# First softmax batch from scores with tokens as rows, and a new order for the first half

## The chip, the cores and the metric

One core of one Trainium2 chip. The metric is the device time of one execution in microseconds (us), lower is better. Three runs of the kernel before gave 615.01, 616.36 and 616.61 us, median 616.36. The core has TensorE (PE in the profile, with PEld for its weight loads), VectorE (DVE), ScalarE (ACT), GpSimd (POOL) and SyncE (SP, which here only issues transfers).

## The reference

Attention between 512 tokens and 32 states in both directions, for 8 batches of 8 heads, then a two-layer network with softplus on all 4608 rows:

```python
scores = scale * np.matmul(x, state.transpose(0, 1, 3, 2))
scores = scores - scores.max(-1, keepdims=True)
a = np.exp(scores)
a /= a.sum(-1, keepdims=True) + 1e-09
xread = np.matmul(a, state)
scores2 = scale * np.matmul(state, x.transpose(0, 1, 3, 2))
scores2 = scores2 - scores2.max(-1, keepdims=True)
a2 = np.exp(scores2)
a2 /= a2.sum(-1, keepdims=True) + 1e-09
sread = np.matmul(a2, x)
...
h = x @ w_in
g = np.maximum(h, 0.0) + np.log1p(np.exp(-np.abs(h)))
return (g @ w_out).astype(np.float32)
```

In the last three lines `x` is `xread` and `sread` with heads side by side: rows of 512, `w_in` 512 x 2048, `w_out` 2048 x 512. Batch 0 is `b == 0` below.

## The kernel before, in words

The first layer is folded into the attention: instead of `xread @ w_in` the kernel makes V = state x w_in once per batch (step v, `v_product`, L370) and multiplies it with the softmax weights `a` (step g, `gemm1`, L635). To do so it needs `a` with the pair (head, state) on the partitions and the tokens along the free axis. The scores (step Q, `scores`, L431) come out of TensorE in that form too: 32 states of 4 heads on 128 partitions, one bank of PSUM for even heads (e = 0), one for odd heads, 512 tokens along. The softmax of the tokens against the states, though, wants its maximum and sum over the 32 states of a head, so the steps of the first softmax go there and back:

- step 1, `a_turn` (L450): VectorE transposes blocks of 32 x 32 from PSUM into SBUF, so that the states lie along the free axis;
- steps 2 to 6: maximum (`a_max`, VectorE), subtraction (`a_sub`), exponential (`a_exp`, ScalarE), sum, epsilon and reciprocal (`a_sum`, VectorE), multiplication (`a_mul`); subtraction and multiplication are given to VectorE or GpSimd by a table;
- step 7, `a_back` (L497): VectorE transposes the blocks back.

Batch 0 goes in two halves of 256 tokens, because its tokens are loaded in two halves. The second softmax (over tokens, steps e, f, i, t, u) reads the same score banks: maximum on VectorE, exponential on ScalarE (step f), transposes by TensorE against an identity matrix (step t, `b<-ident,s` in rows), copies (u).

Batch 0 takes its first four tiles of 128 columns of the hidden layer (F1) in full float32 (`b<-s,s` in rows; TensorE does such a product in two passes, which the trace records as two matmuls), and its first two tiles of the second layer as well (`b<-d,s` of 128x512). All others are split into a high and a low part (steps h/l for V, 8/9 for `a`, m/n for the softplus, D/E for `w_out`) and take three passes in float32r. Weights come as 8-byte words: `a`, `b`, `c` (ScalarE, ScalarE or VectorE, VectorE) make float32 of the ten pieces of `w_in` and put it into the tile `W`; A, B, C do the same for `w_out`. From batch 1 on the second layer takes seven products of half-size slabs instead of eight (steps U, W, Y, F, H, L, M, k, q; M is the product on TensorE), whose weights are written to DRAM (j, K) and read back (J).

The order of everything is a string, PLAN (L43), of 1758 steps: a loop at L999 takes its letters one after the other and runs the next turn of that step, and the order in which instructions are issued is kept on every engine. The table ENG (L67) says for each turn of the steps that may run on more than one engine which one takes it. No engine overtakes within its own queue: an instruction that waits holds back all behind it. SyncE issues all loads and stores in one queue. Buffers are rooms of fixed sizes (`Rooms`), free again after a set number of uses: the r2 rooms are `s`, r4 `d`, r8 `g`, r1 `v`, the eight PSUM banks `b`.

Of the kernel before, what the change touches and what calls it, by code (L numbers as in the profile page):

```python
# [20 lines left out]
P = 128  # L21
# [23 lines left out]
    "1GB93elalGm9gCEgjnADanbEcGfgCGDsimbGIsGsEB4GcvAhjRUmWnS2CjhAlgnOGDlYGaKKgrg3EmsgmjTbBacBnnGCGGAsgjGjbC5Ocssjsv"
    "hjvmTUDGmEGlhlh4WhDdnlnAgYE5GUlBGjgKsOmnG6K7GmG6snQvWCYhDGAjleGjjj7hjlGmKEmj8Kg8SBgs991fnmGGgTCjDUntjnTJsjijWs"
    "tmgeGsUjYEGg1usj2fnGGuGKWoUoj2XtvjKvKpUWuhlQGoY1gshYJgseKogsghW2lsgYHKljsggghlsgsggUsKKfWLgsgsMsFXes3KiJ3FKYHs"
    "R4XFpyzHHLFKFrFMLHZLLHkpMJ5kJMHkJq4JLk5MMLJMkHLH6XJkH7PMR6vvFL7kHJrL8T98hMF9lJhMlhk1g2kgslkHghfsvlvLH3qysgL3h4"
    "lzhsPhLklgXMsghJsgglgH5ssLXJ4gsklqZggJHsMLsJqkgF5ggJssgMss6HkqMFsFkLtuHJFM6LHML7JMTFqH7tF8MkLPJMHkuLHJJM9dJRHP"
    "kvikLkvphFhLkyrkMqzPHXq8HJll9MhlJLLHgJLMZFkHMPhqLkslgkkJkkMHMvskhvQylPhJlggPsq1g2efgzPqskggesJLsqsgh1Hg3sZglhL"  # L50
    "M2ssXfJM3ltHkPkgF4gs5sgggssLsiJJFHs4HLFJ5MMLH6LuMFJJFHMFL6tvkFukHhLlvRP7HHPLhJrkqq8HkLlq7hhMJL9qJJMTH8kMJllMTJ"
    "XPLFqHLqkk9HLMMgggMMsHsskkqkkkLkJPPJJPTJJXPvQv1khhql2qlee13ggggssshsHfhf42llLgggMgggsHFqL35sss4ssgggMsssH56F6k"
    "LFHkLFH7MMttyF8HqFLu7L9kuzHkLFMJPJPJJMMMJJPPJPPRvHZkkHFqLiLkHh8vMMkLlrHhHhHqLlLlkkH9LLqMJXPTJPPJJJJMgMggMssshk"
    "kHkklkkvvQge1hfsgggshsshH2Lll3h1l2leLFgggg4sssfsggggssssgMMM3FHFqsH4F5FqqLH5Lqk6LTPPJJJPMtytMMJJXJHFFHkLiuk7kH"
    "HHHzL6HLqLZkukLMMkFMvvRJJPh8hH7kLqlq9LrqLh8MMMJTJPXJJJPPXJPl9kHkhkkklgMMskklkvQvgghqHl1ehe2sfhfLlh13lqgggssss4"
    "Lq253qgggwiMyPssgHs45MgJzlsgFPLstkuJgkxsgssgtgsMH6sqL7H86PuMFZRLvvkrFJkhlvhlPvhhFFJHFLhlh97MHLlHHMHLMwFkMkHJJ8"
    "hLJJJlPq9MHgLkxsgkgMFsslPwgHgLJqPkLghkMqMgxkHsskgPkskgLJgJgsllqsPLMHLHyzMqZsPwssMkgggqLggskg&P&wsxsxMgkqwkx%%s"
    "wgswx&xqP&%s%s&g%w&wP%wJsxxgwJxxw&x%&%sF&gFw&wx%&%qxg%wHx&s&Lg%H%&sL%&&%s%sHLHLMFHMHFPFJFHHkJFLFLFLLFJkHMLMFJk"
# [4 lines left out]
    '3': "PPPPDPPPDDDPDDDP",  # L63
    '6': "PPPDPPPDDPDDDPPP",
    '8': "DAPPADAAPAAAAADPDD",
    '9': "PPDPDDPDDPDDDPDDPP",
    'B': "DDAADAAA",  # L67
# [1 line left out]
    'E': "DDDDDDPD",
    'F': "DDPDDDDPDDPPDDPDPDPDPPDPDDPDPPDPPDPDPDDDPDPPDPPDDPDDDDPDDDDDDPDD",  # L70
    'H': "AAADAPPAPAPPADDAPAADADAAAAAAAAADPAAAADPAADDAPDAADADDPAADAAAPAPAPAAPADAAAPAPAAAAPADADAADAAAAAAAAPAAAAPAAADAAAAPAA",
    'L': "PDDDDDPDPDDPDDDDDDDDDPPDDDDPDDDDPPPPDPPPPPDDPDDDPDDPDPDDDPDDDPDDDPDDDDPDPDPDDPPDPPPPPPDDDDDDDDDDPDPDPDDDPDDDDPDD",
    'U': "DDPDPDDP",
# [1 line left out]
    'Y': "DDDDPDPD",
    'b': "AAAADDAAAA",
    'h': "AADDDDDAADAAADDDDAADDDDADDADAADDDADDADAADAAAADAAAAADADADADADDAAAAAAA",
    'k': "DADDDDDDDDDDDDDDAADDDDDDDDDDDDDDDADDDDDDDDDDDDDDAADDDDDDDDDDDDDDDDDDDDDDDDDDDDDDAADDDDDDDDDDDDDDAADDDDDDDDDDDDDDDDDDDDDD",
    'm': "PPDADDDAPAAPAA",
    'n': "DDDPDDDDPDPDPP",  # L80
    'o': "AADD",
    'q': "PDDPPDDDPDPDDPPDPPDDDDPPPPPPPDDPDDPPDDDPPPDDPDDDDPPPDPDPDDDD",
    'u': "DAADDAAAADDADDDD",
# [977 lines left out]
```

## Time and profile before

| what | value |
|---|---|
| median of three runs | 616.36 us |
| the profiled execution | 616.66 us |
| its span, first to last instruction | 614.7 us |
| PE busy | 598.5 us (97%) |
| DVE busy | 490.9 us (80%) |
| ACT busy | 267.8 us (44%) |
| POOL busy | 304.9 us (50%) |
| chain that ended last | 92% PE |
| DMA | 161.62 MB, mean 263 GB/s |

A page of the profile gives busy time of each engine, the span in 40 slices of 15.4 us, and the chain of work that ended last, followed back from the end. An engine with idle time costs nothing unless others wait for it; so the waits of the engine that is never idle are what to look for, and then the order of work that leads to each of them. Matmuls overlap, so that a row's time divided by its count is the pace, while the mean duration of one is longer.

### The profile page before, as it was taken

To read this page: it belongs to the slowest core of one execution; us is meant where nothing else is said; L and a number is where in the kernel's file an instruction comes from. 1 tells how busy PE (TensorE), PEld (TensorE's weight loads), DVE (VectorE), ACT (ScalarE), POOL (GpSimd) and SP (SyncE) were. 2 spreads that over 40 slices of the span, in tenths; PEclk is the share of its full clock that TensorE was granted. 3 is DMA by queue.
4 is the path that set the end of the run, shared out by engine and by line. 5 is a ranking of instruction groups with operands and counts; after the bars stand their busy time and mean duration, and the time that the engine had idled before them with its cause. 6 is when DMAs were issued, how large, how long until landed. Compare 5 with 4: busy or idle time off the path is not lost.

```text
span 614.7 us, 10410 instructions
## 1 busy us (share of the span) xinstructions
PE 598.5 (97%) x4048; PEld 485.1 (79%) x4048; DVE 490.9 (80%) x662; ACT 267.8 (44%) x416; POOL 304.9 (50%) x185
## 2 busy tenths in 40 slices
PE   2999999999999999999999999999999999999997
...
PEclk9999999999999999999999999999999999999999
...
GB/s 305 409 407 326 304 303 362 311 344 377 113 307 237 398 334 112 206 292 315 410 105 229 380 323 106 194 382 412 219 155 146 322 208 78 21 244 233 203 310 77
DMA packets 50415, 161.62 MB, mean 263 GB/s; under 512 B 4288, under 2 KB 29376, under 8 KB 37824
## 3 DMA queue, kind: packets, MB, share of 16 engines
...
## 4 chain that ended last, share of the span: by engine, by line
PE 92%; DVE 3%; DMA 3%; issue 1%; POOL 0%; SPq 0%; ACT 0%; POOLq 0%; DVEq 0%; ACTq 0%
PE b L103 92%; DMA slabs<-d 2%; DVE d L103 2%; DMA d<-in_xt_dram 1%; DVE s L103 1%; POOL s L103 0%; DVE v L103 0%; SPq L103 0%; ACT s L103 0%; DVE g L103 0%; DVE W L103 0%; POOLq L103 0%; DVEq L103 0%; ACTq L103 0%
## 5 line engine op out<-in xcount | busy, mean ns | idle before, releaser
L103 PE MATMUL b<-g,d 128*128 128x256 f32 (+1 forms) x1576 | 290.6, 337 | 0.1
L103 PEld LDWEIGHTS b<-g,d 128*128 128x128 f32 x1576 | 246.8, 190 | 36.2 <-POOL d L103 1.1
L103 PE MATMUL b<-d,d 128*128 128x512 f32 x744 | 177.3, 393 | 1.0 <-DVE d L103 1.0
L103 PEld LDWEIGHTS b<-d,d 128*128 128x128 f32 x744 | 137.9, 188 | 32.5 <-issue 2.4
L103 ACT ACTIVATE g<-b 128x512 f32<-128x512 f32 x112 | 66.2, 599 | 141.6 <-PE b L103 132.0
L103 DVE TENSOR_TENSOR s<-s,b 128x512 f32<-128x512 f32 (+1 forms) x105 | 68.7, 675 | 48.0 <-PE b L103 38.7
L103 POOL TENSOR_TENSOR d<-g,d 128x1024 fp32r<-128x1024 f32 x28 | 71.9, 2570 | 46.5 <-ACT d L103 19.6
L103 DVE TENSOR_TENSOR d<-g,d 128x1024 fp32r<-128x1024 f32 x56 | 88.2, 1580 | 3.0 <-ACT d L103 2.7
L103 PE MATMUL b<-g,s 128*128 128x512 f32 (+1 forms) x280 | 70.7, 370 | 0.0
L103 ACT CAST d<-g 128x1024 fp32r<-128x1024 f32 x53 | 55.4, 1052 | 33.5 <-POOL g L103 15.6
L103 PEld LDWEIGHTS b<-g,s 128*128 128x128 f32 x280 | 50.3, 188 | 11.6 <-issue 2.5
L103 POOL TENSOR_TENSOR s<-s 128x256 f32<-128x256 f32 x28 | 31.1, 1114 | 33.5 <-DVE s L103 28.1
L103 DVE TENSOR_TENSOR d<-b,d 128x512 fp32r<-128x512 f32 x62 | 41.6, 682 | 7.3 <-ACT d L103 6.9
L103 POOL TENSOR_TENSOR s<-s,v 128x512 f32<-128x512 f32 x19 | 22.8, 1201 | 44.9 <-DVE v L103 44.3
L103 ACT CAST d<-b 128x512 fp32r<-128x512 f32 x35 | 20.1, 590 | 49.5 <-PE b L103 49.3
L103 POOL TENSOR_SCALAR d<-g 128x1024 fp32r<-128x1024 f32 x17 | 26.6, 1569 | 29.9 <-DVE g L103 19.4
L103 POOL TENSOR_TENSOR g<-g,g 128x1024 f32<-128x1024 f32 x14 | 35.2, 2518 | 10.4 <-DVE d L103 7.7
L103 POOL TENSOR_TENSOR d<-d,d 128x1024 fp32r<-128x1024 f32 (+2 forms) x15 | 30.8, 2055 | 12.7 <-PE b L103 6.4
L103 PE MATMUL b<-W,ST 64*32 64x512 f32 (+2 forms) x544 | 32.7, 577 | 4.1 <-DVE W L103 4.1
L103 DVE TENSOR_TENSOR d<-d,d 128x1024 fp32r<-128x1024 f32 (+2 forms) x27 | 31.4, 1163 | 0.3
L103 DVE COPY s<-b 128x512 f32<-128x512 f32 (+2 forms) x30 | 16.2, 546 | 16.2 <-PE b L103 16.1
L103 ACT COPY s<-b 128x512 f32<-128x512 f32 (+2 forms) x27 | 13.7, 516 | 30.2 <-PE b L103 25.6
...
## 6 DMA issues: line engine op xcount, KB each, us to landing
g<-slabs SPq DMA_DIRECT2D x98, 1024.0 KB, 6.6
d<-in_xt_dram SPq DMA_DIRECT2D x16, 512.0 KB, 6.4
g<-in_w_out_dram SPq DMA_DIRECT2D x8, 1024.0 KB, 15.1
d<-in_xn_dram SPq DMA_DIRECT2D x16, 512.0 KB, 6.8
slabs<-d SPq DMA_DIRECT2D x16, 512.0 KB, 5.8
...
g<-in_w_in_dram SPq DMA_DIRECT2D x6, 1024.0 KB, 15.5
...
```

Of the source, the lines that this page charges most:

```text
L103: return lambda *a, **k: self.tc.keep_in_program_order(f(*a, **k))
```

## The change

For batch 0 the first softmax no longer takes its scores from step Q. Step 1 now makes them a second time on TensorE with the tokens as the stationary side: for each half 8 float32 matmuls, each with 128 tokens of one pair of heads as weights (128 x 128) and the pair's 64 columns of state as moving data. The states then lie along the free axis in a PSUM bank, and VectorE's maximum and subtraction read it there; the four block transposes go. Subtraction for batch 0 is VectorE's always. Back goes the half by four TensorE transposes into a PSUM bank (step 7), which a new step 0 (`a_copy`, on ScalarE by the table) copies to SBUF. The maximum and exponential of the second softmax still read step Q's banks, which therefore have two readers instead of four.

The first half of PLAN is another one (the last 881 letters are the same), and with it the table: counted up to the first M in either string, the steps that the table places stand 35 on POOL, 60 on DVE, 42 on ACT before, and 25 on POOL, 71 on DVE, 48 on ACT now. In the same stretch there are 424 letters before and 445 now. Order of the loads: the fourth `w_in` piece now comes ahead of the second half of batch 1's tokens, the first piece of `w_out` between two of `w_in`, and the first `xn` later.

```diff
 PLAN = (
-    "TSTSIITITIQI1IQ2O3e12e34dfbaafb4c565OOIIOc6vttQvahbuu7cabhXg8chve8Xh7hg9fbag1tahbgg8A8ccsB9sgCgvhguD2hsGsBOIAm"
...
+    "TSTSIITaII1T2Q3I4bQOae1fIebf2Oca3v5td46hc7ba0ihcu5vhQbOegt67Icv1Ohfg08eba9hAuIgahBSctgCbgcggUssgv8hushBm8lnG9s"
...
 ENG = {
...
-    'D': "PDDDPAAA",
...
-    'W': "PAAPPPPA",
...
+    'D': "APAAAADA",
...
+    'W': "AAAAADAD",
...
@@ -216,7 +217,7 @@
     def load_xT():
         for b, i in HALVES:
             if b == 0:
-                t = xT[b, i] = r4.take([P, 4, S // 2])
+                t = xT[b, i] = r4.take([P, 4, S // 2], uses=2)
                 nc.sync.dma_start(t.t, xt[b, :, :, S // 2 * i:S // 2 * i + S // 2])
             else:
                 t = xT[b, i] = r4.take()
@@ -433,8 +434,8 @@
             for u in range(2 if b == 0 else 1):
                 n = S // 2 if b == 0 else S
                 if u == 0:
-                    sc[b, 0], sc[b, 1] = [banks.take(uses=4 if b == 0 else 3) for _ in range(2)]
-                    few[b] = r1.take(uses=3)
+                    sc[b, 0], sc[b, 1] = [banks.take(uses=2 if b == 0 else 3) for _ in range(2)]
+                    few[b] = few.get(b) or r1.take(uses=3)
                 heads([sc[b, e][:, n * u:n * u + n] for e in range(2)], b, lambda q: xT[b, u][:, q] if b == 0 else xT[b, q // 2][:, q % 2])
                 xT[b, u].done()
                 if b:
@@ -447,26 +448,43 @@
     def flat(t):
         return t.rearrange("p a n -> p (a n)")
 
+    turned, back = {}, {}
+
     def a_turn():
         for b, i in KEYS:
-            t = T[b, i] = r2.take([P, 16, NS])
             if b == 0:
-                for e in range(2):
-                    nc.vector.transpose(flat(t[:, 8 * e:8 * e + 8]), sc[b, e][:, span(0, i)])
-                    sc[b, e].done()
+                few[b] = few.get(b) or r1.take(uses=3)
+                t = turned[i] = banks.take(uses=2)
+                for j in range(2):
+                    for q in range(4):
+                        nc.tensor.matmul(t[:, 256 * j:256 * j + 256].rearrange("p (e q n) -> p q e n", e=2, q=4)[:, q],
+                                         xT[b, i][:, q, P * j:P * j + P], ST0[:, 0, q].rearrange("p (e n) -> p e n", e=2),
+                                         start=True, stop=True)
+                xT[b, i].done()
             else:
+                t = T[b, i] = r2.take([P, 16, NS])
                 nc.vector.transpose(flat(t.t), sc[b, i].t)
                 sc[b, i].done()
             yield
 
+    def grouped(t):
+        return t.rearrange("p (a n) -> p a n", n=NS)
+
     def a_max():
         for k in KEYS:
-            nc.vector.tensor_reduce(mx(*k), T[k].t, AX.X, ALU.min if k[0] else ALU.max)
+            nc.vector.tensor_reduce(mx(*k), T[k].t if k[0] else grouped(turned[k[1]].t), AX.X, ALU.min if k[0] else ALU.max)
+            if k[0] == 0:
+                turned[k[1]].done()
             yield
 
     def a_sub():
         for k in KEYS:
-            elementwise(T[k].t, T[k].t, spread(mx(*k)), ALU.subtract, engine())
+            if k[0] == 0:
+                T[k] = r2.take([P, 16, NS])
+                nc.vector.tensor_tensor(T[k].t, grouped(turned[k[1]].t), spread(mx(*k)), ALU.subtract)
+                turned[k[1]].done()
+            else:
+                elementwise(T[k].t, T[k].t, spread(mx(*k)), ALU.subtract, engine())
             yield
 
     def a_exp():
@@ -496,9 +514,22 @@
 
     def a_back():
         for k in KEYS:
-            af[k] = r2.take(uses=4 + F1 if k[0] == 0 else 2)
-            nc.vector.transpose(af[k].t, flat(T[k].t))
+            if k[0] == 0:
+                t = back[k[1]] = banks.take()
+                for e in range(2):
+                    for j in range(2):
+                        nc.tensor.transpose(t[:, 256 * e + P * j:256 * e + P * j + P], flat(T[k].t)[:, 256 * j + P * e:256 * j + P * e + P], ident)
+            else:
+                af[k] = r2.take(uses=2)
+                nc.vector.transpose(af[k].t, flat(T[k].t))
             T[k].done()
+            yield
+
+    def a_copy():
+        for i in range(2):
+            af[0, i] = r2.take(uses=4 + F1)
+            cast(af[0, i].t, back[i].t, engine())
+            back[i].done()
             yield
 
     def part(b, i, e):
@@ -987,7 +1018,7 @@
         "a": win_upper, "b": win_lower, "c": win_join,
         "A": wout_upper, "B": wout_lower, "C": wout_join, "D": wout_hi, "E": wout_lo,
         "v": v_product, "h": v_hi, "l": v_lo,
-        "Q": scores, "1": a_turn, "2": a_max, "3": a_sub, "4": a_exp, "5": a_sum, "6": a_mul, "7": a_back,
+        "Q": scores, "1": a_turn, "2": a_max, "3": a_sub, "4": a_exp, "5": a_sum, "6": a_mul, "7": a_back, "0": a_copy,
         "8": a_hi, "9": a_lo, "e": s_max, "f": s_exp, "i": s_sum, "t": s_turn, "u": s_copy, "R": s_read,
         "r": s_scale, "y": s_back, "z": s_hi, "Z": s_lo,
         "w": w_hi, "x": w_lo, "g": gemm1, "&": h_copy, "%": h_add, "s": softplus, "m": g_hi, "n": g_lo, "G": gemm2,
```

On TensorE, from the program's start to the first product of the hidden layer, before (`b` are PSUM banks, `d0` and `d1` the two halves of batch 0's tokens, `ST0` its states, `ident` the identity; step Q, the products with `W` and batch 1's scores are among the rows left out):

```order
L103 MATMUL b0_1_97<-d0_1_78,ST0_72 32x256
...
L103 MATMUL b4_5_183<-ident_67,s2_3_140 128x128 x4
L103 MATMUL b5_6_188<-ident_67,s6_7_148 128x128 x4
...
L103 MATMUL b2_11_235<-s3_14_224,s9_10_216 128x256
L103 MATMUL b2_11_235<-s3_14_224,s2_17_231 128x256
```

The same stretch of TensorE's queue, from the program's start to the first product of the hidden layer and the transposes behind it, in the changed kernel:

```order
L104 MATMUL b0_1_99<-ST0_72,d0_1_78 128x2x32 x8
...
L104 MATMUL b3_4_142<-ST0_72,d1_2_81 128x2x32 x8
...
L104 MATMUL b6_7_182<-ident_67,s4_5_151 128x128 x4
L104 MATMUL b7_8_194<-ident_67,s1_2_121 128x128 x4
...
L104 MATMUL b4_13_244<-s0_13_203,s9_10_191 128x256
...
L104 MATMUL b7_14_247<-ident_67,s6_7_159 128x128 x4
L104 MATMUL b5_15_253<-ident_67,s8_9_167 128x128 x4
```

The products with the 64 columns of `ST0` (8 for each half) stand ahead of and behind the two halves of step Q, the transposes of batch 0's exponential (`ident` on `s4_5`) are followed by those of its softmax weights (`s1_2`), and of the second half both (`s6_7`, `s8_9`) stand behind the first product of the hidden layer.

On VectorE, from its first instruction on batch 0 on, before (`s0_1` and `s1_2` are the two halves of the first softmax, `v0_1` holds maxima and sums, `SCALAR_TENSOR_TENSOR` into `W` is the join of a weight piece):

```order
L103 STREAM_TRANSPOSE s0_1_110<-b0_1_97 128x256
L103 STREAM_TRANSPOSE s0_1_110<-b1_2_98 128x256
L103 TENSOR_REDUCE v0_1_99<-s0_1_110 128x16
L103 TENSOR_REDUCE v0_1_99<-b0_1_97 128x1
L103 TENSOR_SCALAR v0_1_99<-v0_1_99 128x1
L103 STREAM_TRANSPOSE s1_2_129<-b0_1_97 128x256
L103 STREAM_TRANSPOSE s1_2_129<-b1_2_98 128x256
L103 TENSOR_REDUCE v0_1_99<-s1_2_129 128x16
...
L103 SCALAR_TENSOR_TENSOR W_74<-s4_5_144,s3_4_142 128x4x128
L103 TENSOR_REDUCE v0_1_99<-s0_1_110 128x16
L103 TENSOR_SCALAR v0_1_99<-v0_1_99 128x16
```

VectorE's queue over the same steps in the changed kernel (`s1_2` and `s8_9` are the two halves, `b0_1` and `b3_4` the banks with tokens as rows):

```order
L104 TENSOR_REDUCE v0_1_98<-b0_1_99 128x16
L104 TENSOR_TENSOR s1_2_121<-b0_1_99,v0_1_98 128x512
L104 TENSOR_REDUCE v0_1_98<-b1_2_111 128x1
...
L104 TENSOR_REDUCE v0_1_98<-b3_4_142 128x16
L104 SCALAR_TENSOR_TENSOR W_74<-s0_1_91,s2_3_126 128x4x128
L104 TENSOR_TENSOR s8_9_167<-b3_4_142,v0_1_98 128x512
L104 TENSOR_REDUCE v0_1_98<-s1_2_121 128x16
...
L104 TENSOR_TENSOR s1_2_121<-s1_2_121,v0_1_98 128x512
L104 SCALAR_TENSOR_TENSOR W_74<-s3_4_138,s5_6_157 128x4x128
```

The two transposes in each half are gone, the two subtractions and the first multiplication have come to VectorE, and the first half's sum stands behind the first piece of `W` as before.

On ScalarE, around the first change of its function table, before (`s5_22` is the exponential of batch 1's first bank):

```order
L103 COPY s9_10_216<-b2_3_173 128x128
L103 ACTIVATE s10_11_218<-d6_7_91 128x512
L103 COPY s4_13_222<-b5_6_188 128x512
L103 ACTIVATE s5_15_227<-d8_9_95 128x512
L103 ACTIVATE s7_16_229<-d8_9_95 128x512
L103 COPY s2_17_231<-b3_4_174 128x128
L103 CAST d11_12_255<-s3_14_224 128x256
L103 ACT_TABLE_LOAD
L103 ACTIVATE s5_22_269,v1_2_195<-b6_7_193,v1_2_195 128x512
L103 ACT_TABLE_LOAD
L103 ACTIVATE d14_15_274<-g0_1_108 128x1024
```

ScalarE's queue at the same place in the changed kernel (`s0_13` and `s6_21` are the copies of step 0, `s10_20` is batch 1's exponential):

```order
L104 ACTIVATE s8_9_167<-s8_9_167 128x512
L104 COPY s9_10_191<-b4_5_169 128x128
L104 ACTIVATE s11_12_201<-d7_8_96 128x512
L104 COPY s0_13_203<-b7_8_194 128x512
L104 COPY s4_15_210<-b6_7_182 128x512
L104 COPY s3_16_225<-b0_9_215 128x128
L104 COPY s7_19_275<-b1_10_216 128x128
L104 ACT_TABLE_LOAD
L104 ACTIVATE s10_20_277,v1_2_229<-b2_11_227,v1_2_229 128x512
L104 COPY s6_21_283<-b5_15_253 128x512
L104 ACT_TABLE_LOAD
L104 ACTIVATE d11_12_291<-g0_1_123 128x1024
```

The copy of the second half, which the hidden layer's products of these tokens need, stands behind a table load and batch 1's exponential; the first big piece of weights (`d11_12`) follows another table load, as before.

## Rows read from the trace of the kernel before

**Rows 1.** The profile page: busy times, and two rows of the 40 slices.
```profile
PE 598.5 (97%) x4048; PEld 485.1 (79%) x4048; DVE 490.9 (80%) x662; ACT 267.8 (44%) x416; POOL 304.9 (50%) x185
...
PE   2999999999999999999999999999999999999997
...
PEclk9999999999999999999999999999999999999999
```
**Rows 2.** PE's waits over the span: for whom, us in total, times, longest.
```profile
PE b L103 <- DMA d<-in_xt_dram: 2.2, 1, 2.2
PE b L103 <- DVE d L103: 1.0, 1, 1.0
```
**Rows 3.** Chain that ended last: start us, length us, what.
```profile
96.46 7.62 DMA slabs<-d
...
104.17 0.70 DVE d L103
```
**Rows 4.** Timeline, 0 to 30 us: start, length, engine, operation, count, [idle before <-releaser].
```profile
4.99 1.11 PE L103 MATMUL b<-d,ST 64*32 64x256 f32 x16 [4.99 <-DMA ST<-in_zp_dram]
...
6.17 0.78 DVE L103 STREAM_TRANSPOSE s<-b 128x256 f32<-128x256 f32 x2 [5.31 <-PE b L103]
...
6.99 0.69 DVE L103 TENSOR_REDUCE v<-s 128x16 f32<-128x512 f32 x1
7.76 1.05 POOL L103 TENSOR_TENSOR s<-s,v 128x512 f32<-128x512 f32 x1 [6.45 <-DVE v L103]
...
11.51 1.76 ACT L103 ACTIVATE s<-d 128x512 int32<-128x512 uint8 x3
...
12.74 0.72 DVE L103 SCALAR_TENSOR_TENSOR W<-s,s 128x512 int32<-128x512 int32 x1 [0.17 <-ACT s L103]
...
13.51 0.68 PE L103 MATMUL b<-W,ST 64*32 64x128 f32 x16 [4.10 <-DVE W L103]
...
14.12 1.97 PE L103 MATMUL b<-ident,s 128*128 128x128 f32 x8
...
14.30 0.25 DVE L103 RECIPROCAL v<-v 128x16 f32<-128x16 f32 x1
...
18.62 1.28 ACT L103 ACT_TABLE_LOAD   x1
...
22.18 0.60 PE L103 MATMUL b<-ident,s 128*128 128x128 f32 x4
...
23.06 0.67 DVE L103 TENSOR_SCALAR d<-g 128x1024 int32<-128x1024 int32 x1
23.78 2.36 DVE L103 SCALAR_TENSOR_TENSOR W<-d,d 128x1024 int32<-128x1024 int32 x2
...
28.22 1.96 PE L103 MATMUL b<-d,s 128*128 128x512 f32 x4
```
**Rows 5.** Transfers issued 3.3 to 3.8 us: KB each, us from issue to landing.
```profile
d<-in_w_in_dram SPq DMA_DIRECT2D x1, 512.0 KB, 6.6
```
**Rows 6.** Transfers issued 10.0 to 10.3 us, same columns.
```profile
g<-in_w_out_dram SPq DMA_DIRECT2D x1, 1024.0 KB, 14.6
```
**Rows 7.** Busy us of each engine (instructions) by stretch, then PEclk, DMA share, GB/s.
```profile
13.00:28.00 15.00, 14.49 (x124) 8.95 (x124) 14.18 (x28) 14.26 (x23) 5.38 (x6) 1.00 1.03 408
25.00:50.00 25.00, 25.00 (x178) 16.15 (x177) 24.18 (x36) 24.42 (x30) 7.22 (x8) 1.00 1.03 407
100.00:125.00 25.00, 24.02 (x143) 18.03 (x142) 17.43 (x24) 13.68 (x23) 17.02 (x10) 1.00 0.96 328
125.00:150.00 25.00, 24.93 (x284) 20.92 (x282) 23.41 (x28) 6.76 (x10) 16.22 (x10) 1.00 0.97 376
```
**Rows 8.** Timeline of DVE near 34 us, POOL idle.
```profile
34.00 1.21 DVE L103 TENSOR_TENSOR g<-d,g 128x1024 fp32r<-128x1024 f32 x1
```
**Rows 9.** Timeline near 94 us, DVE and POOL together.
```profile
93.23 1.75 DVE L103 TENSOR_TENSOR g<-d,g 128x1024 fp32r<-128x1024 f32 x1
...
93.98 1.60 POOL L103 TENSOR_TENSOR d<-d,d 128x256 f32<-128x256 f32 x1
```

More of the change, by code (lines that the diff above doesn't have):

```diff
@@ L43 @@
 PLAN = (
-    "TSTSIITITIQI1IQ2O3e12e34dfbaafb4c565OOIIOc6vttQvahbuu7cabhXg8chve8Xh7hg9fbag1tahbgg8A8ccsB9sgCgvhguD2hsGsBOIAm"
[L45 to L58, printed above, removed]
@@ L59 @@
-    "JHLHFkkJMHHLHkLqMHkPLHkFLLJLJHMHLqLJHFkMHPFqkLJLHHkHPFLHMMLJkLMHLHkkkkLJMLqMkPkkHHqPqkqLkqLqPPqMPMkPqMPkqkPP"
+    "TSTSIITaII1T2Q3I4bQOae1fIebf2Oca3v5td46hc7ba0ihcu5vhQbOegt67Icv1Ohfg08eba9hAuIgahBSctgCbgcggUssgv8hushBm8lnG9s"
+    "8lD9GB9fEAG1IAbCDCXgXgA2aGEObm3gBjgOjGanDssGcIGmsWcGvn4CbDmEhlhjRGn5mEBGKsUXrAlOjaYmGcC2AaDBgbUsnngWgGjgKsmScG"
+    "GEiGCGjssnKvmTvjBjjmhDnGlYhnTGlGAgGdhWl3mEhCsgGQn4l5msv67GYjeOmhD6KGJj7Gj18l8jUfh9gEgsKK9BgjsUljWjgAngTYUjGGjs"
+    "egdsg1nK2fWmXCnsGDGjjEsjKmGWnG3KGYGt2iT3YtKosvuKu4ovjXoJhlhXQtouhl4ggjeUsgWsKlghjYUJgssgKgWYssl5gKsKgH56LfgKss"
@@ new lines @@
+    "s1gJHMFJHLseLFFHMRRLf6FFykMMFkHLpkzJHLMrM77pr8qJZ8kpHJHLvkhFl2J9hvM9lg1HJXshg3LgkPiLHMFs2kMXq3kgLlhMskkvsJhPvH"
+    "ylJhLgHhlzH4sgsgLq5HMskgP4ZlgMLh5ystksJgs6gllJJHL7gqsF678JkTLMgP8kggusqs9spMsTMJHFLHtqLgsFMkFJFFJHMkLJMkzvk9vu"
+    "HZHLLXkhJRhHLMlqHPlJhgMkhkFgFLHrMkssllQ1vhPeyTlJJLf2gMHHhzLgHZsMkg3slJ1gLkggHg2sssqsMP4vLeqtJJ3qHHLhfLsgggklss"
+    "5MLMkkkhPJ4t5qPJklsgkgusqu6gssXHH6MgMMvs7FPFPFFHJLJhkhFlviRFqHJMLklLh7H8HMJLMrhF9JMkl8JlLkHkJkMLJPqHMqLJLJkHqM"
+    "TJXPLFqHLqkk9HLMMgggMMsHsskkqkkkLkJPPJJPTJJXPvQv1khhql2qlee13ggggssshsHfhf42llLgggMgggsHFqL35sss4ssgggMsssH56F"
@@ new lines @@
+    "6kLFHkLFH7MMttyF8HqFLu7L9kuzHkLFMJPJPJJMMMJJPPJPPRvHZkkHFqLiLkHh8vMMkLlrHhHhHqLlLlkkH9LLqMJXPTJPPJJJJMgMggMsss"
+    "hkkHkklkkvvQge1hfsgggshsshH2Lll3h1l2leLFgggg4sssfsggggssssgMMM3FHFqsH4F5FqqLH5Lqk6LTPPJJJPMtytMMJJXJHFFHkLiuk7"
+    "kHHHHzL6HLqLZkukLMMkFMvvRJJPh8hH7kLqlq9LrqLh8MMMJTJPXJJJPPXJPl9kHkhkkklgMMskklkvQvgghqHl1ehe2sfhfLlh13lqgggsss"
+    "s4Lq253qgggwiMyPssgHs45MgJzlsgFPLstkuJgkxsgssgtgsMH6sqL7H86PuMFZRLvvkrFJkhlvhlPvhhFFJHFLhlh97MHLlHHMHLMwFkMkHJ"
+    "J8hLJJJlPq9MHgLkxsgkgMFsslPwgHgLJqPkLghkMqMgxkHsskgPkskgLJgJgsllqsPLMHLHyzMqZsPwssMkgggqLggskg&P&wsxsxMgkqwkx%"
@@ L60 @@
+    "%swgswx&xqP&%s%s&g%w&wP%wJsxxgwJxxw&x%&%sF&gFw&wx%&%qxg%wHx&s&Lg%H%&sL%&&%s%sHLHLMFHMHFPFJFHHkJFLFLFLLFJkHMLMF"
+    "JkJHLHFkkJMHHLHkLqMHkPLHkFLLJLJHMHLqLJHFkMHPFqkLJLHHkHPFLHMMLJkLMHLHkkkkLJMLqMkPkkHHqPqkqLkqLqPPqMPMkPqMPkqkPP"
 )
```

41 lines of the change are left out of this document (21 added, 20 removed).

## The prediction

> **What bounds the kernel now.** I read the page first: TensorE is busy 598.5 of 614.7 us, and its row of 40 slices is full in all but the first and the last [rows 1]. So only what ends TensorE's few waits can move the time, and the next view is TensorE's waits. 5.0 us at the start are the first loads, which do not change [rows 4]; 2.2 us are the second half of batch 0's tokens [rows 2]; 4.1 us, up to 13.51, are the first piece of `W` [rows 4]; 1.0 us is an operand written by VectorE [rows 2]. The chain of waits tells what lies behind this last one: a slab's store took from 96.46 to about 104.1, and only then came VectorE's instruction, 0.70 us, that TensorE needed [rows 3]. The timeline of the first 30 us shows how the start ends: VectorE joins two large weight pieces from 23.78 on, and at 28.22 the first product of the second layer begins [rows 4]. I call that moment M. Behind it TensorE is busy 25.00 of 25 us and later 24.02 and 24.93 [rows 7]. The work behind M is the same in both kernels, and the last half of the order as well. So the sum has two terms: how much M moves, and what becomes of the stalls behind it.
>
> **The change, part by part.** *Scores with tokens as rows.* Each half gets 8 float32 products, 16 matmuls in the trace, each with 128 columns to load and 64 to move. No row shows this shape. The nearest are 16 matmuls of step Q with 256 columns in 1.11 us, and transposes with 128 columns, 8 in 1.97 us early and 4 in 0.60 us later [rows 4]. Below, a half costs no less than nothing, since nothing is removed on TensorE; 16 at 0.11 us are 1.7 us, 16 at the early 0.25 us are 3.9 us. I take 3.4, nearer to the early transposes. The first half runs from 4.99, followed by its step Q (1.11): 9.5 at most, beside 8.31 when the other tokens come. The second, with its Q, ends at 11 to 14. The first `W` piece can't be used before about 13, so nearly all of it lies in the 4.1 us wait; the upper end would cost 1 us.
>
> The clock: the granted clock of the page reads 9 or more in every slice, of the full level of 2.4 GHz [rows 1], yet the early transposes, which come after waits of 2.2 and 4.1 us, ran at about half the pace of those at 22.18 [rows 4]. I read the early ones as the 1.2 GHz level. The changed kernel fills both waits in part, so its transposes may run at the faster pace, which gives at most 1 us of slack on TensorE and nothing at M as long as VectorE is last there.
>
> *Transposes back.* Eight on TensorE, 0.60 to 0.98 us for four, one or both halves in the dense part before M; then a copy on ScalarE, about 0.6 us by the three instructions of 128x512 that took 1.76 [rows 4]. Gone from VectorE are two transposes of 128x256 for each half (0.78) and one of 128x512; come to it are two subtractions and a multiplication, which took 1.05 on GpSimd and on VectorE, by the maximum's row, 0.69 each [rows 4]. On VectorE that is 2 x (0.78 + 0.70) off and 3 x 0.69 on, about 0.9 us less by itself; but the new order puts other things ahead of the second large join.
>
> *M.* The first small piece of `w_in` is issued at 3.5 and lands 6.6 us later [rows 5], at 10.1. Two extractions on ScalarE (0.59 each) and an exponential between them of like size bring 11.9, and VectorE's maxima and the join 13.0, where before the wait ended at 13.51. From there VectorE's queue up to the second large join is ten instructions on 128x512 (0.69), eight small ones (at most 0.25, I take 0.2), copies of together 0.9, two half-size lower parts (0.35, half of a large one), three large ones (0.67) and three large joins (1.18) [rows 4]: 6.9 + 1.6 + 0.9 + 0.7 + 2.0 + 3.5 = 15.6. Neighbours overlap a little, so I take 15.4, and the join ends at 28.4. VectorE was busy 14.18 of the 15 us from 13 to 28 before [rows 7], so there is little air in such a queue. TensorE then needs half of a group of sixteen, 0.55: M = 28.95, 0.7 us later than before. Two other chains end earlier. The large `w_in` piece now stands in the load slot that took 14.6 us from 10.0 [rows 6], so it lands at 24.6, and extraction and join could be done by 26.9: that is the lower end, M = 27.5. ScalarE has batch 1's exponential behind VectorE's maximum (about 20.0), then the copy of the second half, a table load of 1.28, and three large extractions of 1.17 (twice the 0.59 of the small) with a copy between: 26.8. This is only 0.4 before VectorE wants the last of them. The upper end is one table load and one exponential late there, 1.97 us: M = 30.9.
>
> *Behind M.* The stall at 104 hung on a store that was issued late. In the new order another instruction stands there; I take the 1.0 us as gone, with nothing and 1.0 as its bounds. GpSimd gets 10 steps fewer, VectorE 11 more up to the first M step of the string. VectorE was busy 24.18 of 25 us from 25 to 50 and 23.41 from 125 to 150 [rows 7], so added work there is a risk; but it runs alone more often, and the same subtraction of 128x1024 took 1.21 us with GpSimd idle [rows 8] and 1.75 with GpSimd beside it [rows 9]. I take the two as even, 0, with 2.2 us lost as the upper bound (four such instructions dearer by 0.54) and nothing gained below, since TensorE hardly waits there.
>
> The Trainium skill ("SBUF — State Buffer", Who interferes with whom) says that a VectorE instruction with two inputs in SBUF contends with a GpSimd instruction that reads SBUF, and that one of them waits altogether. By that rule moving steps away from GpSimd buys back part of what VectorE gains in work: the sum would be a little lower than by counting instructions alone. The trace agrees with 1.75 beside 1.21.
>
> *Sum.* 616.66 (the profiled execution) + 0.7 - 1.0 = 616.4. That execution is 0.3 above the median of 616.36, so against the median I forecast 616.1.
>
> **The rivals.** *A, ScalarE is last at M (slower).* If batch 1's maximum on VectorE comes more than 0.4 us late, the exponential, the copy, the table load and the extractions all slide, and the second join with them. For it: VectorE's full queue [rows 7] and a copy that stands behind an exponential it has nothing to do with. Against it: the maxima and subtraction that read PSUM start before the `W` piece has landed. M at 30.9 and the stall at 104 still there: 616.66 + 2.7 - 0.3 = 619.1.
>
> *B, VectorE overfull later (slower).* The 11 steps more on VectorE, 0.69 to 1.21 us each, are 8 to 13 us, and the place where GpSimd made up for it is 125 to 150, where VectorE had 1.6 us free [rows 7]. It decides if the buffers run dry there. 616.66 + 0.7 - 1.0 + 2.7 - 0.3 = 618.8 (2.7 being five of the dearer instructions).
>
> *C, the start gains (faster).* If VectorE's queue has more overlap than I gave it, M is set by the load, 27.5, and the stall goes: 616.66 - 0.7 - 1.0 - 0.3 = 614.7; tenths more if other pauses inside the dense part, too short for a row here, go as well, so 614.2. For it: the loads that the weights need come earlier in the queue. Against it: the join chain is counted from rows and would have to lose 1.5 us.
>
> *D, only the start is moved and the stall stays (no change).* 616.66 + 0.7 - 0.3 = 617.1; it lies in the forecast's own range.
>
> **How the numbers follow.** The forecast, with D, has 0.47, A 0.18, B 0.10, C 0.25. A difference under 0.3%, 1.85 us, cannot be told from none here, so the bounds are 614.5 and 618.2. C lies about that lower bound and most of it counts as faster, with a little of the forecast's lower end: 0.24. A and B are slower but for their lower edges, and the forecast with D adds its upper edge: 0.28. The rest, 0.48, is the same. The forecast's own range is 615.2 to 617.3. The range for 8 in 10 reaches into C (down to 613.8, M and stall gained with some tenths) and over A's 619.1 to 619.6.
>
> **What would show it right or wrong.** Right: TensorE's first wait for `W` is under 2.5 us; the first product of the second layer begins at 28.5 to 29.4, just behind the second large join on VectorE; no wait of TensorE for the slab store near 104; VectorE's busy sum some us higher and GpSimd's lower. A shows as the second large join with idle time before it, released by ScalarE, and M near 31. B shows as waits of TensorE for VectorE between 125 and 150. C shows as M before 28. Wrong altogether would be a wait of more than 2 us at a place that none of these names.

## The result and the profile after

The changed kernel takes 620.37 us in the median of 5 runs (618.56 to 621.08), the kernel before 616.36 (615.01 to 616.61). The ratio is 1.0066, with a 95% interval of 1.0047 to 1.0084: slower by 4 us, beyond the forecast's range for 8 in 10, which ended at 619.6. The profiled execution took 620.37 us, its span is 618.4 against 614.7 before.

TensorE's timeline of the changed kernel from the start to M (start us, length us, engine, operation, count, idle time before and what ended it):

```profile
5.04 3.65 PE L104 MATMUL b<-ST,d 128*128 128x64 f32 x16 [5.04 <-DMA ST<-in_zp_dram]
8.62 1.96 PE L104 MATMUL b<-d,ST 64*32 64x256 f32 x32
10.51 3.67 PE L104 MATMUL b<-ST,d 128*128 128x64 f32 x16
15.57 0.68 PE L104 MATMUL b<-W,ST 64*32 64x128 f32 x16 [1.38 <-DVE W L104]
...
17.99 1.12 PE L104 MATMUL b<-ident,s 128*128 128x128 f32 x4 [0.69 <-DVE s L104]
...
21.34 2.07 PE L104 MATMUL b<-s,s 128*128 128x256 f32 x4
23.21 1.41 PE L104 MATMUL b<-ident,s 128*128 128x128 f32 x8
...
25.14 1.99 PE L104 MATMUL b<-s,s 128*128 128x256 f32 x8
...
31.82 1.33 PE L104 MATMUL b<-W,ST 64*32 64x512 f32 x16
33.07 3.27 PE L104 MATMUL b<-d,s 128*128 128x512 f32 x7
```

M is at 33.07, 4.85 us later than the 28.22 of [rows 4]. Step v begins at 15.57 instead of 13.51, 2.06 later, and from v to M go 17.50 us instead of 14.71, 2.79 more. The waits of TensorE over the whole span (for whom, us in total, times, longest), and the long unbroken piece of the chain of waits (start, length, what):

```profile
PE b L104 <- DMA ST<-in_zp_dram: 5.0, 1, 5.0
PE b L104 <- DVE W L104: 1.4, 1, 1.4
PE b L104 <- DVE s L104: 0.7, 1, 0.7
```

```profile
17.99 107.50 PE b L104 x660
```

The 4.1 us for `W` have become 1.4, the 2.2 for the tokens are gone, since the turns fill them, and the 1.0 us for VectorE at 104 [rows 2] does not show any more: the span is 3.7 longer, not 4.85. But the waits that went were filled with work that took longer than the waits. VectorE and then ScalarE, timeline, same columns:

```profile
8.73 0.69 DVE L104 TENSOR_REDUCE v<-b 128x16 f32<-128x512 f32 x1 [7.86 <-PE b L104]
...
14.22 0.69 DVE L104 TENSOR_REDUCE v<-b 128x16 f32<-128x512 f32 x1 [1.88 <-PE b L104]
14.83 0.68 DVE L104 SCALAR_TENSOR_TENSOR W<-s,s 128x512 int32<-128x512 int32 x1
...
17.24 0.69 DVE L104 TENSOR_TENSOR s<-s,v 128x512 f32<-128x512 f32 x1
...
23.06 0.70 DVE L104 STREAM_TRANSPOSE s<-b 128x512 f32<-128x512 f32 x1
...
27.73 1.23 DVE L104 SCALAR_TENSOR_TENSOR W<-d,d 128x1024 int32<-128x1024 int32 x1 [1.00 <-ACT d L104]
...
30.80 1.23 DVE L104 SCALAR_TENSOR_TENSOR W<-d,d 128x1024 int32<-128x1024 int32 x1
```

```profile
23.86 0.69 ACT L104 ACTIVATE s<-b,v 128x512 f32<-128x512 f32 x1 [1.95 <-DVE s L104]
...
24.65 0.59 ACT L104 COPY s<-b 128x512 f32<-128x512 f32 x1
25.25 1.28 ACT L104 ACT_TABLE_LOAD   x1
26.55 2.21 ACT L104 ACTIVATE d<-g 128x1024 f32<-128x1024 f32 x2
```

VectorE's maximum of the second half starts at 14.22, when TensorE's second turn is done, and the first join, which stands behind it in VectorE's queue, at 14.83 (12.74 in [rows 4]). Behind that stand the subtraction, the sum and the multiplication (17.24) for which TensorE waits at 17.99, so this wait too goes back to the end of the second turn. Further on the first large join had waited 1.00 us for ScalarE, whose exponential of batch 1 began at 23.86, 0.1 behind the end of VectorE's transpose of the same bank. Behind that exponential ScalarE copies the second half of the softmax weights (step 0, 24.65), loads a table and makes the extraction (26.55) that the first large join takes. TensorE's last products with `W`, begun at 31.82, stop in their middle for the second large join, which ends at 32.03, and M comes 1.04 behind it. The page's busy sums:

```profile
PE 607.7 (98%) x4088; PEld 494.4 (80%) x4088; DVE 480.0 (78%) x662; ACT 263.5 (43%) x413; POOL 304.3 (49%) x182
```

TensorE's busy time rose by 9.2 us, VectorE's fell by 10.9, GpSimd's hardly moved [rows 1].

### The profile page after: what moved, and what is told of

Same layout as the page of the kernel before. It is cut to its first block, busy times and chain, and to the rows that moved or that the text cites. A ratio compares the mean times of both kernels' runs of the same rounds, so it can differ in the third digit from the quotient of the medians.

```text
span 618.4 us, 10470 instructions
## 1 busy us (share of the span) xinstructions
PE 607.7 (98%) x4088; PEld 494.4 (80%) x4088; DVE 480.0 (78%) x662; ACT 263.5 (43%) x413; POOL 304.3 (49%) x182
## 4 chain that ended last, share of the span: by engine, by line
PE 96%; DMA 2%; DVE 2%; POOL 0%; SPq 0%; issue 0%; POOLq 0%
PE b L104 96%; DMA g<-slabs 1%; DVE g L104 1%; DMA ST<-in_zp_dram 1%; DVE s L104 0%; POOL d L104 0%; DVE v L104 0%; DVE d L104 0%; SPq L104 0%; DVE W L104 0%; POOLq L104 0%
## 5 line engine op out<-in xcount | busy, mean ns | idle before, releaser
L104 POOL TENSOR_TENSOR d<-g,d 128x1024 fp32r<-128x1024 f32 x32 | 82.0, 2566 | 64.2 <-PE b L104 40.2
L104 DVE TENSOR_TENSOR d<-g,d 128x1024 fp32r<-128x1024 f32 x52 | 86.7, 1671 | 14.7 <-ACT d L104 14.3
L104 ACT CAST d<-g 128x1024 fp32r<-128x1024 f32 x50 | 52.1, 1052 | 40.5 <-POOL g L104 23.3
L104 DVE TENSOR_TENSOR d<-b,d 128x512 fp32r<-128x512 f32 x62 | 41.8, 681 | 10.5 <-ACT d L104 10.3
L104 POOL TENSOR_SCALAR d<-g 128x1024 fp32r<-128x1024 f32 x20 | 29.8, 1492 | 38.5 <-DVE g L104 29.7
L104 ACT CAST d<-b 128x512 fp32r<-128x512 f32 x38 | 21.8, 589 | 51.2 <-PE b L104 45.8
L104 POOL TENSOR_TENSOR s<-s 128x256 f32<-128x256 f32 x28 | 29.8, 1068 | 20.3 <-DVE s L104 20.3
L104 POOL TENSOR_TENSOR s<-s,v 128x512 f32<-128x512 f32 x11 | 13.4, 1216 | 44.0 <-DVE v L104 36.8
L104 POOL TENSOR_TENSOR g<-g,g 128x1024 f32<-128x1024 f32 x10 | 26.0, 2604 | 10.3 <-DVE d L104 7.7
L104 DVE TENSOR_TENSOR d<-d,d 128x1024 fp32r<-128x1024 f32 (+2 forms) x26 | 29.1, 1120 | 0.5
L104 POOL TENSOR_TENSOR d<-g 128x1024 f32<-128x1024 f32 x6 | 15.2, 2528 | 25.8 <-ACT g L104 25.1
```

The lines of the kernel that those rows point to most:

```text
L104: return lambda *a, **k: self.tc.keep_in_program_order(f(*a, **k))
```

## The experiments

Start of step v, M and time of every run; the ratio is to the kernel before on the same chip. M is read from the one profiled execution.

| run | v | M | median us | ratio, 95% |
|---|---|---|---|---|
| before | 13.51 | 28.22 | 616.36 | |
| changed | 15.57 | 33.07 | 620.37 | 1.0066 (1.0047 to 1.0084) |
| e1 before, waits filled | 13.04 | 28.15 | 616.90 | 1.0025 (1.0012 to 1.0039) |
| e2 join first | 14.01 | 32.37 | 619.88 | 1.0068 (1.0051 to 1.0085) |
| e3 old order, new softmax | 17.01 | 36.45 | 625.56 | 1.0169 (1.0140 to 1.0199) |
| e4 new order, old softmax | 13.09 | 31.43 | 618.55 | 1.0048 (1.0033 to 1.0063) |
| e5 early products | 18.11 | 33.29 | 617.49 | 1.0026 (1.0011 to 1.0041) |
| e6 turns in one pass | 11.85 | 29.41 | 617.02 | 1.0020 (1.0004 to 1.0035) |
| e7 before, other room | 13.51 | 28.23 | 615.41 | 0.9991 (0.9979 to 1.0003) |
| e8 early products, join first | 12.64 | 30.22 | 617.97 | 1.0035 (1.0018 to 1.0053) |
| e9 back twice | 15.85 | 34.25 | 621.61 | 1.0084 (1.0060 to 1.0108) |
| e10 second turn in one pass | 13.58 | 31.13 | 618.63 | 1.0042 (1.0029 to 1.0055) |
| e11 first turn in one pass | 13.79 | 31.16 | 618.81 | 1.0041 (1.0023 to 1.0058) |
| e12 one pass, filled | 12.10 | 29.54 | 616.87 | 1.0017 (1.0004 to 1.0030) |
| e13 exponential first | 15.50 | 32.94 | 620.32 | 1.0071 (1.0050 to 1.0092) |
| e14 e12 with e13 | 12.71 | 28.55 | 615.98 | 0.9997 (0.9987 to 1.0007) |

**Softmax or order: e3 and e4.** In e3 the old string gets a `0` behind each of the first two `7` and the old table; in e4 the new string loses both `0` and its first `Q` goes ahead of the first `1`:

```
e3:  -7   +70      (twice, old PLAN, new functions)
e4:  -II1T2Q3I4bQ   +IITQ123I4bQ   -0 -0   (new PLAN, old functions)
```

> The order of before with the new softmax of batch 0 (scores with tokens as rows, transposes back on TensorE, copies on ScalarE behind them). Theory 1 (the added work on TensorE and the later first join): TensorE runs from 4.99 to 14.0 without a pause, v starts at about 15.5, M at 32 to 33.5, the stall at 104 stays, 620.5 to 621.5 us. Theory 3 (the new order alone costs the time): M near 28.5 to 29.5, 616.4 to 617.5 us.

> The new order with the old softmax of batch 0 (block transposes on VectorE; the first step Q moved ahead of the first step 1, no step 0). Theory 1: M at 28 to 29, the stall at 104 gone, 615.3 to 616.3 us. Theory 3: M at 31 to 33, 618.5 to 620 us.

e3 lies outside what either theory gave: the new softmax in the old order is the worst of all (M at 36.45). e4 came where theory 3 had it: the new order alone is slow too (31.43). So neither theory holds alone. TensorE in e3, then in e4 (timeline as above):

```profile
10.57 3.67 PE L104 MATMUL b<-ST,d 128*128 128x64 f32 x16
17.01 0.68 PE L104 MATMUL b<-W,ST 64*32 64x128 f32 x16 [2.77 <-DVE W L104]
...
36.45 4.10 PE L104 MATMUL b<-d,s 128*128 128x512 f32 x9
```

```profile
13.09 0.68 PE L104 MATMUL b<-W,ST 64*32 64x128 f32 x16 [3.65 <-DVE W L104]
...
16.11 0.68 PE L104 MATMUL b<-W,ST 64*32 64x128 f32 x16 [1.30 <-DVE W L104]
...
22.13 0.64 PE L104 MATMUL b<-W,ST 64*32 64x256 f32 x8 [0.69 <-DVE W L104]
...
31.43 5.42 PE L104 MATMUL b<-d,s 128*128 128x512 f32 x12
```

In e3 v starts at 17.01, though the second turn ends at about 14.2: more stands between the turn and the join there. In e4 v starts early, 13.09, but TensorE then waits three times for `W`, and VectorE's queue holds the transposes of the old softmax again; that these are the cause is not shown by itself. So of the 8.2 us that the new softmax costs in the old order, the new order recovers 3.4, and it costs 3.2 by itself.

**Is TensorE what holds M in the kernel before: e1.** A step that takes a bank, issues products and gives the bank back is put behind each of the first two `Q` (its loop and `yield` are left out here):

```
+ t = banks.take(); banks.free.appendleft(t.tag)
+ for _ in range(FILLS.pop(0)):    # 2, then 4
+     nc.tensor.matmul(t.t[:, 0:256], ident, xT[0, 0][:, 0], start=True, stop=True)
```

> The kernel before, with float32 products of the identity and tokens (256 columns, results unused) put on TensorE in its two early waits: two behind the first half of step Q, four behind the second. M is the start of the second layer's first product, 28.22 before. Theory 1 (TensorE's own unbroken stretch from the first W piece to M sets M, half of it at the lower level): the clock is up earlier than 17.9, M comes at 26.5 to 27.3 and the time falls by 1 to 1.7 us. Theory 2 (VectorE's joins of W set M): the second large join stays near 26.1, M at 27.9 to 28.3, no change of time.

```profile
13.43 1.09 PE L104 MATMUL b<-ident,s 128*128 128x128 f32 x8
...
17.57 1.10 PE L104 MATMUL b<-s,s 128*128 128x256 f32 x4 [0.85 <-DVE s L104]
...
28.15 5.42 PE L104 MATMUL b<-d,s 128*128 128x512 f32 x12 [0.39 <-DVE d L104]
```

The transposes behind v take 1.09 us where they took 1.97 [rows 4], so the clock is up earlier (the trace records its rise at 8.42 us), and M stays: theory 1 falls for the kernel before. TensorE only gets new waits for VectorE (0.85 and 0.39). The time is 0.25% above the kernel before, clear of its interval, which neither theory had; the profiled execution, with a span of 614.6 us beside 614.7, does not show where.

**The join behind the maximum: e2.**

```
- bf2Oca3v5
+ bfcO2a3v5
```

> The changed kernel with the join of the first W piece ahead of the maximum of batch 0's second half on VectorE. Theory 1: the join no longer waits for TensorE's second turn (14.2), so step v starts at 14.2 instead of 15.57, the wait of 1.4 us is gone, M moves from 33.07 to about 32.4 and the time falls by about 0.6 us. Theory 2: v starts at 14.2 as well, but M stays at 33.0, because the second large join waits for ScalarE's extraction.

```profile
17.41 1.12 PE L104 MATMUL b<-ident,s 128*128 128x128 f32 x4 [1.67 <-DVE s L104]
```

v starts at 14.01 and M is at 32.37, as theory 1 had it. The start of v gains 1.56, M only 0.70: TensorE's transposes back of the first half now wait 1.67 for VectorE. A gain in time does not show (1.0068 against the changed kernel's 1.0066, with intervals wider than the 0.6 us expected), and TensorE's waits have a new one of 0.9 us for GpSimd, which theory 1 didn't foresee.

**How long the turns take: e6, e10, e11.** The turn reads the upper halves of the words; in e10 the second half alone, in e11 the first alone:

```
+ def top(ap):
+     return ap.bitcast(bfloat16).rearrange("p (n two) -> p n two", two=2)[:, :, 1]
- xT[b, i][:, q, P * j:P * j + P], ST0[:, 0, q].rearrange(...)
+ top(xT[b, i][:, q, P * j:P * j + P]), top(ST0[:, 0, q]).rearrange(...)
```

> The changed kernel with the turn's 16 products made from the upper halves of the float32 words (bfloat16, one pass instead of two), so that batch 0's first softmax comes from truncated scores; nothing is done about the clock. A turn should take about half, 1.7 to 1.9 us. Theory 4: the second turn ends at 10.5 to 11, v starts at 13 to 13.5, M at 29.5 to 31 (TensorE's other early work stays at the lower level), time 616.3 to 618. Theory 5: M above 31.4, time above 618.5.

> The changed kernel with only the second half's turn in one pass, from truncated words; the first turn stays at 3.65 us. Theory 4 (the end of the second turn, with the maximum and the join behind it, sets v and M): it ends near 11, v at 12.5 to 13, M at 29.9 to 30.6. Theory 8 (what counts is the late first half: its maximum at 8.73 instead of 5.8): M above 32.

> The changed kernel with only the first half's turn in one pass, from truncated words. Theory 4: the second turn, at full length, ends at 12.1 to 12.6, v at 13.4 to 13.9, M at 30.5 to 31.3. Theory 8: M at 29.4 to 29.9, as with both turns short.

TensorE in e6, e10 and e11:

```profile
4.91 0.58 PE L108 MATMUL b<-ST,d 128*128 128x64 bf16 x8 [4.91 <-DMA ST<-in_zp_dram]
...
8.36 0.61 PE L108 MATMUL b<-ST,d 128*128 128x64 bf16 x8
11.85 0.68 PE L108 MATMUL b<-W,ST 64*32 64x128 f32 x16 [2.88 <-DVE W L108]
...
29.41 5.42 PE L108 MATMUL b<-d,s 128*128 128x512 f32 x12
```

```profile
10.51 0.61 PE L112 MATMUL b<-ST,d 128*128 128x64 bf16 x8
13.58 0.69 PE L112 MATMUL b<-W,ST 64*32 64x128 f32 x16 [2.47 <-DVE W L112]
```

```profile
13.79 0.68 PE L112 MATMUL b<-W,ST 64*32 64x128 f32 x16 [1.38 <-DVE W L112]
```

A short turn of either half brings v 1.8 to 2.0 and M 1.9 us forward, both together 3.72 and 3.66. From v to M stay 17.4 to 17.6 us each time. So the length of the turns counts by way of the second turn's end and v (theory 4), and what v gains M gains; that the late first half alone counts (theory 8) is wrong. It does not count in full: each shortened turn is 3.1 us shorter. In e10 the second maximum and the join then stand in VectorE's own queue without a wait, and in e11 the second half starts only when its tokens have landed (TensorE waits 1.15 us for them). e11 came where theory 4 had it; e10's v and M were 0.5 us later than expected, e6's v 1.2 earlier, the one-pass turn being shorter than half.

**The clock: e5, e8, e12.** Nine products `matmul(t, ident, ident)` at the head of the program and four of e1's behind the second turn (e5), the same with e2's edit (e8), and three of e1's behind e6's second turn (e12).

> The changed kernel with 9 float32 products of the identity with itself on TensorE before the first loads land (from about 1.4 us), and 4 products of the identity with tokens (256 columns) behind the second turn; results unused. Theory 4 (the two turns run at the lower level of the clock, and what waits behind the second, the maximum and the first join, is what makes M late): if the clock is up when the turns run, each takes 1.8 us instead of 3.65, the second ends at 10.5 to 11, step v starts at 13 to 13.5 instead of 15.57, M at 29 to 30.5, time 616 to 617.5 us. Theory 5 (behind the first join the queues of VectorE and ScalarE are too full anyway): v starts early as well but M stays above 31.4, time above 618.

> The changed kernel with the early products as in the run before last but two, and the join of the first W piece ahead of the second maximum. Theory 4: v starts near 13, M 29 to 30, time 615.7 to 617. Theory 5: the join was hardly held back any more, so the same as with the early products alone, M above 31.4.

> Both turns in one pass from truncated words, and three products of the identity with tokens (256 columns, results unused) in TensorE's wait behind the second turn. If the clock goes up by 13 instead of 19, TensorE's stretch up to M gets about 2 us shorter: by theory 6 M comes at 27.5 to 28.2 and the time is 0.1 to 0.2% below the kernel before; by theory 7 M stays at 29.0 to 29.4 and the time 0.1 to 0.2% above it.

```profile
8.80 2.00 PE L106 MATMUL b<-ST,d 128*128 128x64 f32 x16
...
12.64 0.45 PE L106 MATMUL b<-W,ST 64*32 64x128 f32 x16
...
15.62 0.66 PE L106 MATMUL b<-ident,s 128*128 128x128 f32 x4 [1.95 <-DVE s L106]
...
30.22 5.42 PE L106 MATMUL b<-d,s 128*128 128x512 f32 x12
```

```profile
12.51 0.65 PE L110 MATMUL b<-ident,s 128*128 128x128 f32 x4
14.42 0.75 PE L110 MATMUL b<-ident,s 128*128 128x128 f32 x4 [1.26 <-DVE s L110]
...
29.54 5.42 PE L110 MATMUL b<-d,s 128*128 128x512 f32 x12
```

e5's profiled execution took 620.60 us where the run's median is 617.49; in it the clock had not risen when the turns ran (3.64 and 3.67 us), so its M says nothing on a risen clock. The median lies at the upper end of what theory 4 gave; what the faster executions did was not profiled. In e8 the clock had risen: the second turn took 2.00 us, v came at 12.64 and M at 30.22. In e12 it had by 12.51, and M stayed where e6 had it. But in both TensorE then waits for VectorE's multiplication (1.95 and 1.26 us), and behind that wait the granted clock falls again, to 0.50 (e8 from 17 to 18 us, e12 from 15 to 18), while batch 1's scores run. These scores also stop in their middle for the second half of batch 1's tokens, which the new order loads later: it lands at 16.70 in e8 and 16.23 in e12 (15.41 in the kernel before; 16.79 in the changed kernel, where the scores begin only at 19.46). So these runs do not isolate the clock. In e12 VectorE's maximum of batch 1, at 18.26, waits 0.52 us for the scores; clock and load together hold it back by no more than that, and the rest is the queues of VectorE and ScalarE. e8's M is nearer to theory 4, but its time of 617.97 is above what that gave; e12 came out close to theory 7, M 29.54 and 0.17% above the kernel before.

**From v to M: e9, e13, e14.** e9 issues each transpose back twice. e13 moves one letter, so that ScalarE's exponential of batch 1's first bank comes ahead of VectorE's transpose of that bank; e14 puts that edit into e12:

```
e9:  - for e in range(2): for j in range(2): transpose(...)
     + for e, j in [(e, j) for _ in range(2) for e in range(2) for j in range(2)]: transpose(...)
e13: - Icv1Ohfg08eba9
     + IcvOhfg08e1ba9
```

> The changed kernel with each of the eight transposes back issued twice into the same place. Theory 6 (from 17.99 on M is set by TensorE's own unbroken stretch): 0.85 us more for the first four at the lower level and 0.45 to 0.85 for the second, M at 34.4 to 34.8, time up by 1.3 to 1.7. Theory 7 (VectorE's and ScalarE's queues hold M): M at 33.0 to 33.6, time up by less than 0.5.

> The changed kernel with VectorE's transpose of batch 1's first score bank put behind ScalarE's exponential of the same bank (and behind the next maximum) instead of ahead of it. In the changed kernel that exponential begins at 23.86, 0.1 us behind the transpose's end, with its maximum done at 22.4. Theory 9 (the two readers of one bank run in the order of the program, and ScalarE's late exponential, copy, table load and extraction hold the large joins): the exponential begins at 22.5, the first large extraction at 25.2 instead of 26.55, and VectorE's idle 1.0 us before the first large join goes. If ScalarE's queue alone held M: M at 31.7 to 32.2, time 0.9 to 1.4 below the changed kernel. If TensorE's own stretch (17.99 to 33.07) holds M as well: M at 32.7 to 33.1, time less than 0.4 below it.

> Both turns in one pass from truncated words, three filling products behind the second turn, and the exponential ahead of the transpose as in the kernel beside it. Here TensorE waits for the joins at the end of its stretch, so by theory 9 M comes at 28.3 to 28.8 instead of 29.54 and the time falls by 0.7 to 1.2 us against the same kernel without it (to about 615.6 to 616.2). If the joins are held by loads or by VectorE's own queue, M stays at 29.3 or more.

TensorE in e9, ScalarE in e13, ScalarE in e12 and in e14:

```profile
18.27 1.97 PE L104 MATMUL b<-ident,s 128*128 128x128 f32 x8 [0.69 <-DVE s L104]
```

```profile
22.46 0.69 ACT L104 ACTIVATE s<-b,v 128x512 f32<-128x512 f32 x1 [0.62 <-DVE v L104]
...
24.51 0.58 ACT L104 COPY s<-b 128x512 f32<-128x512 f32 x1 [1.27 <-PE b L104]
```

```profile
20.46 0.69 ACT L110 ACTIVATE s<-b,v 128x512 f32<-128x512 f32 x1 [1.66 <-DVE s L110]
```

```profile
19.42 0.69 ACT L110 ACTIVATE s<-b,v 128x512 f32<-128x512 f32 x1
```

e9, of two runs, starts 0.28 late and has M 1.18 later, 0.9 net. That lies between the two theories' numbers, and it is what TensorE's own time grew by: 0.85 for the first set (1.97 for eight against 1.12 for four) and 0.07 for the second, which shares its row with four others (1.48 for twelve against 1.41 for eight, the pace having doubled in it). In e13 the exponential goes to 22.46, as theory 9 said, and nothing is won: ScalarE's copy of the second half then waits 1.27 us for TensorE's transposes of that half, to 24.51 instead of 24.65, and M stays (32.94, in a program whose v is 0.07 earlier). In e14, where these transposes come early, the same letter brings ScalarE's exponential from 20.46 to 19.42 and M from 29.54 to 28.55. VectorE's maximum of batch 1 begins at 18.26 in both, so the gain is the letter's. The time goes from 1.0017 to 0.9997 of the kernel before, with intervals that overlap.

So in the changed kernel two chains of nearly equal length meet at ScalarE's copy of the second half: TensorE's unbroken stretch, whose transposes it reads, and the queues of VectorE and ScalarE with the late exponential; one has to shorten both. From the copy on there is one chain, by the table load, the extraction and the large joins. In every version with the new order M is 2.27 or 2.28 us behind the start of the second large join: 30.80 and 33.07 in the changed kernel, 31.98 and 34.25 in e9, 30.67 and 32.94 in e13, 27.27 and 29.54 in e12, 26.28 and 28.55 in e14.

**The stall at 104: e7.** The kernel before with two free rooms of the `d` kind exchanged at one take:

```
+ if self.shape == [P, 2, 512] and self.made == 77:
+     self.free[0], self.free[1] = self.free[1], self.free[0]
```

> The kernel before with one room swapped: the cast at 104.17 writes another free room of the same size, whose last reader was VectorE itself, instead of the one that a store still reads. If the stall at 104 costs its 1.0 us to the end, TensorE's wait for VectorE there is gone, M stays at 28.2 and the time falls by 0.9 to 1.2 us (ratio 0.998 to 0.9985). If the same time is given back at a later wait, the time stays.

The kernel before, then e7:

```profile
105.73 1.62 PE L103 MATMUL b<-d,d 128*128 128x512 f32 x6 [0.98 <-DVE d L103]
```

```profile
104.59 5.62 PE L103 MATMUL b<-d,d 128*128 128x512 f32 x24
```

The products that began at 105.73 in the kernel before begin at 104.59, without a wait, M is unchanged, and the span is 613.7, 1.0 less. The timed ratio of 0.9991 is on the side that was expected, but its interval takes in 1. It is the only exact version here that ends below both kernels in the median; e14 equals the kernel before, with scores from truncated words.

## Why the prediction was wrong

- **What bounds the kernel** was named rightly: TensorE's stretch behind M is the same, and only M and the stalls count. M moved by 4.85, the span by 3.7. From M to the end of the span it is 585.3 to 585.7 us in the changed kernel and ten of the versions, and 586.2 to 586.5 in the kernel before, e1, e2, e3 and e8, each of which has a further wait of 0.8 to 1.0 us behind M.
- **The price of the turn** was near: 3.4 us a half forecast, 3.65 measured. The lower price of 0.11 us a matmul stands in no row; e8's second turn, at the fast pace, took 2.00 us, 0.125 a matmul. The step that failed is the next one: "nearly all of it lies in the 4.1 us wait", with the join at 13.0. That wait was TensorE's, but the second turn is also what VectorE's maximum waits for, and the first join stands behind that maximum. The join ended at 15.51, where the forecast had 13.0: 2.5 of the 4.1 us by which M was missed (28.95 forecast). In e6, e10 and e11 M follows v one to one.
- **From the join to M** the forecast counted VectorE's queue without a pause, 15.4 us to the end of the second large join and 0.55 behind it. It took 16.52, of which VectorE waited 1.00 for ScalarE, as rival A had it, for the reason it gave (batch 1's maximum began at 21.53, where the forecast had about 20.0). Behind the join it took 1.04. Together these are the other 1.6 us. But e13 shows that the late exponential alone doesn't hold ScalarE back: TensorE's stretch, on whose transposes ScalarE's copy waits, does so too, with 0.69 of waiting for the multiplication, the transposes back (1.12 for the first four) and more work at the slow pace: four products of 128x256 took 2.07 where later eight took 1.99. I had taken TensorE for idle enough here, though the rows had it busy 14.49 of 15 us from 13 to 28 [rows 7].
- **The clock.** "Nothing at M as long as VectorE is last there" was right for the kernel before (e1). In the changed kernel the pace doubled at about 24, before at about 18, and that is part of TensorE's longer stretch; how much by itself wasn't isolated. So filling the waits did not bring the faster pace to the transposes, as the forecast thought it might.
- **The stall at 104**: 1.0 was forecast as gone; 4.85 less 3.7 is 1.15, and e7 takes 1.0 off the span by that stall alone. This term was right.
- **The busy sums**: VectorE's was forecast some us higher and fell by 10.9, GpSimd's was forecast lower and hardly moved. Nothing hung on it, since TensorE waits for neither behind M.
- **Rival A** had the sign and the mechanism, at 0.18, and a price of 2.7 at M, too small since it left the first join at 13.0. **Rival B** did not come: TensorE was busy 25.00 of 25 us from 100 to 125 and 24.91 from 125 to 150 (24.93 in [rows 7]), and no wait for VectorE shows there. **Rival C** needed an early v, and in **rival D** the stall stays, which it did not.
- The rule of the Trainium skill on shared ports that was weighed ("SBUF — State Buffer", Who interferes with whom) has nothing to decide here: behind M the span gained 1.15 us, of which the stall is 1.0.
